# Exponentials on VectorE as four phase-shifted linear-mantissa terms, summed by the value matmul, in an attention and spectral mix

## The chip, the cores and the metric

The kernel runs on one core of a Trainium2 chip. The metric is device time in microseconds; "the time before" is the median of three runs. One profiled execution of the same kernel gives the rows below; its own time is shown beside its span.

## The reference

Two branches over the same 2048 x 448 input are mixed by a gate: softmax attention with 16 heads of width 28, and a filter in the Fourier domain.

```python
def _A_ref(x, wqkv, wo):
    H = 16; Dh = D // H                       # D = 448, S = 2048
    qkv = (x @ wqkv).reshape(B, S, 3, H, Dh)  # transposed to q, k, v of b h s d
    scores = einsum("bhqd,bhkd->bhqk", q, k) * Dh ** -0.5
    o = einsum("bhqk,bhkd->bhqd", softmax(scores), v)
    return o.reshape(B, S, D) @ wo
def _B_ref(x, w_r, w_i):
    return irfft2(rfft2(x) * (w_r + 1j * w_i))
g = sigmoid((A_x * gate_w).sum(-1))
out = g * _A_ref(A_x, ...) + (1 - g) * _B_ref(B_x, ...)
```

## The kernel before

**Tiling.** The heads are taken in four groups g of four (heads lie in 32-row strips of the 128 partitions), and the queries in four blocks c of 512. Each pair n = (g, c) is a stage; there are 16. In a stage, 16 key tiles kt of 128 keys times four heads give 64 units, a unit being the scores of one key tile and head, 128 x 512. Four units of one key tile are called a quad. The queries and keys are scaled so that a score is the logarithm to base 2 times 512 (`UNITS`), and a row of each carries half the squared norm, so that no maximum has to be subtracted; the weights `w` put that back into V.

**Who computes which exponential.** `ND[n]` quads of stage n go to VectorE (27 quads in all), the rest to ScalarE. ScalarE works in steps of three and two units, alternating between the PSUM tiles `psA` and `psB` (line 1033), and writes bf16 into a `ring` of 30 slots. VectorE's quads are "dunits": a score matmul into one of two background PSUM banks `bg`, an addition that makes a 16-bit integer `y4` of it (line 969), and when all four are there, a cubic in the mantissa over the whole quad, 128 x 2048, in seven operations (`g1` to `g7`, lines 976 to 998), the last of which writes a `pd` tile. `y4` has two buffers, `pd` four; `dF` and `dW` one.

**Value matmul.** In `attention`, the quads of a stage are read in pairs: eight matmuls (four heads, each in its own 32 output rows) accumulate into one PSUM bank `pvb`, with `vw` (V times `w`, one column for the row sum) as weights. VectorE's quads stand together, ahead of the last two of the stage. A ring slot is free again when the pair that reads it has run. After the stage, `normalise` evicts the bank (line 1124), sends the row sums through a DMA (`rs`), takes the reciprocal, sends it back in rows by two DMAs (`r8`), spreads it over the partitions by a matmul, and multiplies.

**Order of the work.** All instructions are collected as `Op`s with an engine, an assumed duration, dependencies, a due time (`key`) and a release time. `Sched.run` plays them through a list schedule and the program is emitted in the planned order, which each engine then follows strictly. Scores for ScalarE come first on PE; other PE work (projections, V blocks, the Fourier branch, out-projection, all through the two `bg` banks) goes between them by due time. Where PE would stand idle, `fill` puts a matmul of zeros into a free `bg` bank or, while a value accumulation is open, adds zeros to `pvb`; only while the busy share in a sliding stretch of the plan (`HAMW`) is under `HAMF`. DMAs go through SP's queue in the planned order, POOL sets and pads weights and casts the row-sum columns of `vw` (line 870). `proj_group`, `w_block` and `v_block` make keys, queries, `w` and `vw` of a group during the stage before it.

## Time and profile before

| | |
|---|---|
| time, median of 3 runs | 488.3 us (485.94 to 495.7) |
| profiled execution, its own time | 483.99 us |
| its span, first to last instruction | 482.2 us |
| mean granted TensorE clock | 0.943 of full speed |
| PE / VectorE / ScalarE / POOL busy | 425.6 / 401.2 / 423.8 / 22.5 us |

The span is cut by the profile into instructions of each engine. Idle time of an engine is put down to what ended it. A busy PE is not a PE at its peak, since the ends of pipelined matmuls are modelled; durations of neighbours on one engine overlap a little, so the distance between starts is the better measure of pace. The granted clock is the share of the 2.4 GHz that PE got: 0.5 is the level of 1.2 GHz.

### The profile page before, as it was taken

The numbers are of one execution on the slowest core, as the hardware profiler recorded it, in microseconds if no ns is written. First come the engines' busy times: TensorE is split into PE (matmuls) and PEld (weight loads), VectorE is DVE, ScalarE is ACT, GpSimd is POOL, SyncE is SP. The second block draws the span as 40 slices with busy tenths as digits, with TensorE's granted clock in tenths as the row PEclk, the third lists the DMA queues.
The fourth block names the chain that finished last, engine by engine and source line by source line (L and its number), as shares of the span: only waits on it lengthen the run. The fifth ranks groups of instructions, "written<-read, shape, count | busy, mean of one in ns | idle before, by whom it ended". The sixth has DMA issues, their size and how long they took to land.

```text
span 482.2 us, 8537 instructions
## 1 busy us (share of the span) xinstructions
PE 425.6 (88%) x3271; PEld 156.5 (32%) x3271; DVE 401.2 (83%) x682; ACT 423.8 (88%) x390; POOL 22.5 (5%) x58
## 2 busy tenths in 40 slices
PE   6899899898988799988888898999899889998876
PEld 3433223223443222233333333223244332322222
DVE  2555788579889968999999999799998989999732
ACT  2679999779999969999999989689999979999950
POOL 6600000000000000000000000000000000000000
PEclk9989999759999958999999999599999999999998
DMA  9110011001100211121111100000000000010011
GB/s 249 18 34 28 4 27 48 3 0 26 26 1 16 55 23 24 32 48 40 24 26 33 28 12 2 12 1 13 24 16 13 24 22 24 24 42 28 12 40 38
DMA packets 28361, 13.98 MB, mean 29 GB/s; under 512 B 18176, under 2 KB 27936, under 8 KB 28320
## 3 DMA queue, kind: packets, MB, share of 16 engines
q1 hardware_dynamic: 27216, 13.09, 10.9%
q8 instruction: 25, 0.41, 0.4%
q10 hardware_dynamic: 1104, 0.35, 0.3%
q14 instruction: 16, 0.13, 0.1%
HBM read 11.21 MB, written 1.84 MB: 27 GB/s over the span
## 4 chain that ended last, share of the span: by engine, by line
ACT 38%; PE 28%; DVE 15%; issue 13%; DMA 4%; SPq 2%; ACTq 0%; DVEq 0%
ACT ring L1033 37%; PE bg L508 13%; PE psA L508 5%; PE pvb L508 5%; PE psB L508 4%; DVE y L969 2%; SPq L490 2%; PE bg L511 2%; DVE dW L984 1%; DMA k<-nrow 1%; DMA U<-in_A_wqkv_dram 1%; DVE dF L976 1%; DMA r<-rhl 1%; DMA rs<-pvs 1%; DVE pvs L1124 1%
## 5 line engine op out<-in xcount | busy, mean ns | idle before, releaser
L1033 ACT ACTIVATE ring<-psA 128x1536 bf16<-128x1536 f32 (+1 forms) x184 | 283.8, 1542 | 22.7 <-PE psA L508 16.4
L1033 ACT ACTIVATE ring<-psB 128x1024 bf16<-128x1024 f32 x183 | 205.6, 1124 | 6.9 <-PE pvb L508 4.2
L508 PEld LDWEIGHTS <-k 32*128 32x128 bf16 x1024 | 49.5, 91 | 154.7 <-issue 142.7
L508 PE MATMUL psA<-q,k 32*128 32x512 bf16 x550 | 76.9, 400 | 25.6 <-ACT ring L1033 22.0
L508 PE MATMUL psB<-q,k 32*128 32x512 bf16 x366 | 75.3, 397 | 6.7 <-ACT ring L1033 5.3
L969 DVE TENSOR_SCALAR y<-bg 128x512 uint16<-128x512 f32 x108 | 72.2, 682 | 6.9 <-PE bg L508 6.5
L508 PE MATMUL pvb<-ring,vw 128*32 128x512 bf16 x916 | 73.4, 400 | 0.5 <-DVE pvs L1124 0.5
L508 PE MATMUL bg<-q,k 32*128 32x512 bf16 x108 | 40.3, 399 | 1.2 <-DVE k L810 0.3
L984 DVE TENSOR_TENSOR dW<-dF,dW 128x2048 f16<-128x2048 uint16 x27 | 32.8, 1214 | 0.1
L995 DVE TENSOR_TENSOR y<-y,dW 128x2048 uint16<-128x2048 uint16 x27 | 32.7, 1212 | 0.0
L991 DVE TENSOR_TENSOR dW<-dW,dF 128x2048 f16<-128x2048 f16 x27 | 32.6, 1208 | 0.1
L508 PEld LDWEIGHTS <-vw 128*32 128x32 bf16 x1024 | 17.0, 95 | 32.6 <-issue 29.2
L1228 DVE CAST U<-bg 113x512 bf16<-113x512 f32 x32 | 21.5, 682 | 3.6 <-PE bg L508 3.2
L508 PE MATMUL bg<-R,X 128*113 128x256 bf16 x128 | 23.9, 290 | 0.2 <-DVE y L969 0.2
L508 PEld LDWEIGHTS <-xT 128*128 128x128 bf16 x320 | 18.5, 97 | 16.1 <-issue 14.3
L870 POOL CAST vw<-w 128x16 bf16<-128x16 f32 x16 | 7.4, 466 | 342.2 <-ACT w L865 342.2
L508 PE MATMUL bg<-xT,wpk 128*128 128x512 bf16 (+1 forms) x60 | 22.6, 478 | 0.6 <-DVE xT L780 0.3
L810 DVE TENSOR_SCALAR k<-bg,cst 128x512 bf16<-128x512 f32 x15 | 11.2, 749 | 13.7 <-PE bg L508 13.7
L508 PE MATMUL bg<-xT,wpq 128*128 128x512 bf16 (+1 forms) x60 | 19.7, 415 | 0.4 <-DVE q L810 0.2
L1160 DVE SCALAR_TENSOR_TENSOR fin<-bg,gs,xtok 128x448 bf16<-128x448 f32 x16 | 10.9, 680 | 10.9 <-PE bg L508 10.8
L508 PE MATMUL bg<-Bd,xT 128*128 128x450 bf16 x64 | 17.2, 357 | 2.1 <-DVE X L1203 1.0
L976 DVE TENSOR_SCALAR dF<-y 128x2048 uint16<-128x2048 uint16 x27 | 18.5, 686 | 0.3
(97 smaller groups left out, 475.8 us busy)
## 6 DMA issues: line engine op xcount, KB each, us to landing
RB<-cRB SPq DMA_DIRECT2D x16, 128.0 KB
Wg<-in_B_w_i_dram SPq DMA_DIRECT2D x32, 56.2 KB
xtok<-in_A_x_dram SPq DMA_DIRECT2D x4, 448.0 KB
out_dram<-fin SPq DMA_DIRECT2D x16, 112.0 KB
CS<-cCS SPq DMA_DIRECT2D x16, 96.0 KB
Wg<-in_B_w_r_dram SPq DMA_DIRECT2D x16, 56.2 KB
r<-rhl SPq DMA_DIRECT2D x32, 4.0 KB
U<-in_A_wqkv_dram SPq DMA_DIRECT2D x2, 252.0 KB
```

What stands on the lines that cost most here:

```text
L490: self.pin(e.dma_start(out=out() if callable(out) else out, in_=in_() if callable(in_) else in_))
L508: self.pin(self.nc.tensor.matmul(out, lhsT=lhsT, rhs=rhs, start=start, stop=stop, **kw))
L511: self.pin(self.nc.tensor.transpose(out=out, in_=in_, identity=self.c("ident")[0:n, 0:n]))
L810: self.pin(nc.vector.tensor_scalar(out=dst, in0=self.bgi(it), scalar1=self.sv, scalar2=None, op0=ALU.mult))
L969: self.pin(nc.vector.tensor_scalar(out=ys[:, s, :], in0=self.bgi(it), scalar1=127 * UNITS + 1.5, scalar2=0.0, op0=ALU.add, op1=ALU.max))
L976: self.pin(nc.vector.tensor_scalar(out=fl(self.dF), in0=fl(ys), scalar1=511, scalar2=None, op0=ALU.bitwise_and))
L984: self.pin(nc.vector.tensor_tensor(out=fl(self.dW), in0=fl(self.dF), in1=fl(self.dW), op=ALU.mult))
L991: self.pin(nc.vector.tensor_tensor(out=fl(self.dW), in0=fl(self.dW), in1=fl(self.dF).bitcast(F16), op=ALU.mult))
L995: self.pin(nc.vector.tensor_tensor(out=fl(ys), in0=fl(ys), in1=fl(self.dW), op=ALU.add))
L1033: self.pin(nc.scalar.activation(out=self.ring[:, u0:u0 + len(st), :], in_=slot[:, 0:len(st), :], func=ACT.Exp, scale=LN2 / UNITS))
L1160: self.pin(nc.vector.scalar_tensor_tensor(out=fin[:], in0=self.bgi(it)[:, 0:D], scalar=self.gs[:, t:t + 1], in1=self.bm[:, t, 0:D], op0=AL ...
L1228: self.pin(nc.vector.tensor_copy(out=dst, in_=src))
```

## The change

VectorE's exponential no longer corrects the mantissa by a cubic. The integer y, read as a floating-point number, is a linear interpolation of the exponential between powers of two. The change makes four such numbers from each quad, with y shifted by 0, 129, 258 and 387 of 512 units (`PHASE`), and lets the value matmul sum all four, with weights `vd` that are `vw` times a gain for each phase (`PHGAIN`). So a VectorE quad costs four wide operations where there were seven, and is read four times by PE where it was read once. In detail:

- `ND` becomes 0, then 2 fourteen times, then 1: 29 quads where there were 27.
- The phases of a stage's quads are spread over the stage by `self.elems`; the first comes after three quads in the first stage of a group, else after one. `pd` gets six buffers, `dF` and `dW` go.
- `vd` (for the last three key tiles, `DKT`) is made once for a group: `v_block` for the last block evicts part of the tile in f32 to `vf` by a second VectorE operation, POOL copies the weights' column and makes four products. These wait for the last phase matmul of the group before.
- The weights of group 3 (`wpad`) share the tile of group 0, and are padded after its projections.
- `fill` uses at most 256 columns, a limit of 0.7 where it was 0.62, and may write the value bank between its eviction and the next stage, and, as it did, while it is open. The prologue's fillers become 20 of 256 columns.
- Due times: `DUE_P`, and `SWP` names a constant that stays 1.0.

```diff
-EXPA, EXPB = 0.29727136, 0.09245069
+PHASE = (0, 129, 258, 387)
+PHGAIN = [2.0 ** (-d / UNITS) / (4 * 1.0406815) for d in PHASE]
+NPD, DKT = 6, 3
...
-HAMW, HAMF = 3.4, 0.62
+HAMW, HAMF = 3.4, 0.7
...
-            n = min(512, int((gap - SWITCH) * 2400.0) // 32 * 32)
+            n = min(256, int((gap - SWITCH) * 2400.0) // 32 * 32)
...
             elif pvopen[0]:
+                target = None
+            elif pvopen[1] is not None and pvopen[1].end is not None and pvopen[1].end + LAT["DVE"] <= t:
+                target = -1
+            elif pvopen[1] is not None and pvopen[1].end is None:
                 target = None
...
-    ND = [0] + [1] * 2 + [2] * 12 + [1]
+    ND = [0] + [2] * 14 + [1]
...
-        self.dF = T([P, 4, 512], U16, "dF")
-        self.dW = T([P, 4, 512], F16, "dW")
-        self.pd = [T([P, 4, 512], BF16, f"pd{i}") for i in range(4)]
+        self.pd = [T([P, 4, 512], BF16, f"pd{i}") for i in range(NPD)]
+        self.vd = T([P, 4, DKT, 4, 32], BF16, "vd")
+        self.vf = T([P, DKT, 4, DH + 1], F32, "vf")
...
+        for i in range(20):
+            self.pe(256, lambda: self.mm(self.psA[:, 2, 0:256], self.zero[:, 0:P], self.zero[:], True, True),
...
+        elif bank < 0:
+            self.mm(self.pv[:, 0:n], self.zero[:, 0:P], self.zero[:, 0:n], True, True)
...
+        lo = 4
+        if b == 3:
+            alld = min(len(self.dk[4 * g + c]) for c in range(4))
+            lo = 4 - min(alld, DKT)
...
-        e = self.dve(0.54, fe, [ops[-1], wop[0], self.vms[g], ("vwar", g)] + pre, due - 1.5, free=it)
+        e = self.dve(0.07 + lo * .117, fe, [ops[-1], wop[0], self.vms[g], ("vwar", g)] + pre, due - 1.5,
+                     free=it if b < 3 else None)
+        if b == 3:
+            def fd():
+                src = free_dims(self.bgi(it), [[m, DKT], [DH, 4], [1, DH]], m * (4 - DKT))
+                wv = free_dims(self.w[g][:], [[4, DKT], [1, 4], [0, DH]], 16 * b + 4 * (4 - DKT))
+                self.pin(nc.vector.tensor_tensor(out=self.vf[:, :, :, 0:DH], in0=src, in1=wv, op=ALU.mult))
+            e2 = self.dve(0.07 + DKT * .117, fd, [e] + getattr(self, "vdprev", []), due - 1.4, free=it)
+
+            def fw():
+                self.pin(nc.gpsimd.tensor_copy(out=self.vf[:, :, :, DH:DH + 1],
+                                               in_=free_dims(self.w[g][:], [[4, DKT], [1, 4], [1, 1]],
+                                                             16 * b + 4 * (4 - DKT))))
+            pw = self.pool(0.2, fw, [wop[0]] + getattr(self, "vdprev", []), due)
+            self.vdops[g] = []
+            for f in range(4):
+                def fp(f=f):
+                    self.pin(nc.gpsimd.tensor_scalar(out=self.vd[:, f, :, :, 0:DH + 1], in0=self.vf[:],
+                                                     scalar1=PHGAIN[f], scalar2=None, op0=ALU.mult))
+                self.vdops[g].append(self.pool(0.6, fp, [e2, pw, self.vdms], due))
+            self.vdready[g] = self.vdops[g][-1]
+            self.vdprev = self.vdops[g]
...
+        for n in range(16):
+            quads = [("a", kt) for kt in self.ak[n]]
+            na, ph = len(quads), [("d", kt, f) for kt in self.dk[n] for f in range(4)]
+            lo = 3 if n % 4 == 0 else 1
+            el = []
+            for i, q in enumerate(quads):
+                while ph and lo + (na - 2.0 - lo) * (4 * len(self.dk[n]) - len(ph)) / (4 * len(self.dk[n])) <= i:
+                    el.append(ph.pop(0))
+                el.append(q)
+            el[-1:-1] = ph
+            self.elems.append(el)
...
+                due = fdue[0] - DUE_P + 0.6 * s
+                m = sc.op("PE", 0.22, fm, self.kev[g, kt // 4] + self.qev[g, c], due - 1, rel, "row", it, name="dunit")
...
-                    self.pin(nc.vector.tensor_scalar(out=ys[:, s, :], in0=self.bgi(it), scalar1=127 * UNITS + 1.5,
+                    self.pin(nc.vector.tensor_scalar(out=ys[:, s, :], in0=self.bgi(it), scalar1=127 * UNITS,
                                                      scalar2=0.0, op0=ALU.add, op1=ALU.max))
-                p1s.append(self.dve(0.61, f1, [m, prevy], due - 12, free=it))
...
-            def g1(ys=ys):
-                self.pin(nc.vector.tensor_scalar(out=fl(self.dF), in0=fl(ys), scalar1=511, scalar2=None,
-                                                 op0=ALU.bitwise_and))
...
-            def g2():
-                self.pin(nc.vector.tensor_scalar(out=fl(self.dW), in0=fl(self.dF), scalar1=-512.0, scalar2=1.0 / 512,
-                                                 op0=ALU.add, op1=ALU.mult))
...
-            def g3():
-                self.pin(nc.vector.tensor_tensor(out=fl(self.dW), in0=fl(self.dF), in1=fl(self.dW), op=ALU.mult))
...
-            chain = p1s + [prevt]
-            for j, (fn, dur) in enumerate([(g1, .61), (g2, .61), (g3, 1.14), (g4, .61), (g5, 1.14), (g6, 1.14)]):
-                o = self.dve(dur, fn, chain, due - 4 + j * .3, name="dexp")
-                chain = [o]
-            o = self.dve(0.61, g7, chain + [pvdep.get(di - 4)], due, name="dexp")
-            self.dlast[di] = o
-            self.pdops[n, kt] = (o, pds, di)
+                p1s.append(self.dve(0.61, f1, [m, prevy], due, free=it, name="dp1"))
...
+            for f in range(4):
...
+                pds = self.pd[j % NPD]
...
+                def g1(ys=ys, pds=pds, f=f):
...
+                    self.pin(nc.vector.tensor_scalar(out=fl(pds).bitcast(U16), in0=fl(ys), scalar1=float(PHASE[f]),
+                                                     scalar2=0.25, op0=ALU.add, op1=ALU.mult))
+                o = self.dve(0.61, g1, p1s + phs[-1:], fdue[f], name="dexp")
+                phs.append(o)
+                pdseq.append((o, n, kt, f))
+                self.pdops[n, kt, f] = (o, pds, j)
...
-            quads = [("a", kt) for kt in self.ak[n]]
-            dqs = [("d", kt) for kt in self.dk[n]]
-            pos = len(quads) - 2
-            quads[pos:pos] = dqs
+            quads = self.elems[n]
...
+                            if kind == "a":
+                                rhs, lw = self.ring[:, self.unit_slot[n, kt, s][0], :], self.vw[g][:, kt, s, :]
+                            else:
+                                rhs = self.pdops[n, kt, f[0]][1][:, s, :]
+                                lw = self.vd[:, f[0], kt - (NT - DKT), s, :]
+                            self.mm(self.pv[32 * s:32 * s + 32, :], lw, rhs,
```

## Rows read from the trace of the kernel before

**Rows 1.** The page's first part: busy time, share of the span, instructions.

```profile
PE 425.6 (88%) x3271; PEld 156.5 (32%) x3271; DVE 401.2 (83%) x682; ACT 423.8 (88%) x390; POOL 22.5 (5%) x58
```

**Rows 2.** The timeline of ScalarE: start, duration (us), instruction, idle time before it.

```profile
314.60 1.02 ACT L1033 ACTIVATE ring<-psB 128x1024 bf16<-128x1024 f32 x1 [3.12 <-PE pvb L508]
...
455.07 1.52 ACT L1033 ACTIVATE ring<-psA 128x1536 bf16<-128x1536 f32 x1
...
457.31 1.54 ACT L1033 ACTIVATE ring<-psA 128x1536 bf16<-128x1536 f32 x1
...
464.01 0.77 ACT L1033 ACTIVATE ring<-psA 128x512 bf16<-128x512 f32 x1
```

**Rows 3.** Busy by stretch: length, PE, PEld, DVE, ACT, POOL, clock, DMA share, GB/s.

```profile
36.00:90.00 54.00, 49.70 (x377) 16.30 (x374) 39.77 (x66) 52.95 (x49) 0.51 (x2) 1.00 0.10 25
90.00:108.00 18.00, 17.66 (x78) 3.81 (x79) 11.35 (x16) 12.29 (x11) 0.00 (x0) 0.53 0.00 1
108.00:168.60 60.60, 52.21 (x482) 22.30 (x481) 55.81 (x101) 60.60 (x59) 1.71 (x4) 1.00 0.11 25
168.60:183.00 14.40, 14.37 (x64) 3.09 (x63) 9.56 (x16) 9.97 (x9) 0.00 (x0) 0.53 0.09 19
183.00:301.40 118.40, 103.63 (x862) 40.41 (x858) 116.27 (x212) 115.05 (x106) 2.81 (x4) 0.99 0.12 27
301.40:314.00 12.60, 12.60 (x60) 3.89 (x62) 10.04 (x16) 8.29 (x7) 0.00 (x0) 0.51 0.04 12
314.00:466.00 152.00, 136.66 (x1114) 49.47 (x1107) 138.47 (x222) 145.10 (x132) 1.82 (x4) 1.00 0.08 22
```

**Rows 4.** Waits of ScalarE: total us, times, longest us.

```profile
ACT ring L1033 <- PE pvb L508: 10.2, 6, 3.1
```

**Rows 5.** The timeline of all engines around one wait for the ring.

```profile
269.42 0.61 PE L508 MATMUL pvb<-ring,vw 128*32 128x512 bf16 x8
...
280.10 0.63 DVE L998 TENSOR_SCALAR pd<-y 128x2048 uint16<-128x2048 uint16 x1
...
281.61 0.61 PE L508 MATMUL pvb<-pd,vw 128*32 128x512 bf16 x8
...
282.96 1.45 ACT L1033 ACTIVATE ring<-psA 128x1536 bf16<-128x1536 f32 x1 [2.29 <-PE pvb L508]
```

**Rows 6.** Groups by line: tiles, shapes, count, busy us, mean ns, idle before.

```profile
L969 DVE TENSOR_SCALAR y<-bg 128x512 uint16<-128x512 f32 x108 | 72.2, 682 | 6.9 <-PE bg L508 6.5 <-PE psB L508 0.3
...
L984 DVE TENSOR_TENSOR dW<-dF,dW 128x2048 f16<-128x2048 uint16 x27 | 32.8, 1214 | 0.1
...
L976 DVE TENSOR_SCALAR dF<-y 128x2048 uint16<-128x2048 uint16 x27 | 18.5, 686 | 0.3
```

**Rows 7.** The timeline of PE at full clock, one value op and its successor.

```profile
46.69 0.61 PE L508 MATMUL pvb<-ring,vw 128*32 128x512 bf16 x8
...
47.23 0.39 PE L508 MATMUL psA<-q,k 32*128 32x512 bf16 x3
```

**Rows 8.** Busy time by stretch, matmuls of zeros alone (fillers).

```profile
36.00:90.00 54.00, 0.00 (x0) 0.00 (x0) 0.00 (x0) 0.00 (x0) 1.00 0.10 25
...
sum 430.00, PE 21.57 PEld 5.93 ACT 0.00 POOL 0.00; mean PE 3.08 PEld 0.85 ACT 0.00 POOL 0.00
```

**Rows 9.** The timeline of PE's weight loads where the first slow stretch begins.

```profile
90.01 0.10 PEld L508 LDWEIGHTS <-cst 8*128 8x128 bf16 x1 [1.67 <-DMA r<-rhl]
```

**Rows 10.** Groups by line of POOL, the widest copy.

```profile
L598 POOL COPY wpq<-U 128x336 bf16<-128x336 bf16 x3 | 1.4, 466 | 0.3 <-DMA U<-in_A_wqkv_dram 0.3
```

**Rows 11.** The timeline of VectorE: a value bank's eviction, the last V block's.

```profile
365.45 0.68 DVE L1124 COPY pvs<-pvb 128x512 f32<-128x512 f32 x1
...
373.26 0.62 DVE L902 TENSOR_TENSOR vw<-bg,w 128x448 bf16<-128x448 f32 x1
```

**Rows 12.** The timeline of POOL: two of the sixteen equal casts.

```profile
38.05 0.25 POOL L870 CAST vw<-w 128x16 bf16<-128x16 f32 x1 [8.45 <-ACT w L865]
...
245.90 1.13 POOL L870 CAST vw<-w 128x16 bf16<-128x16 f32 x1 [5.89 <-ACT w L865]
```

More of the change, by code (lines that the diff above doesn't have):

```diff
@@ L153 @@
 SWITCH = 0.1
-HAMW, HAMF = 3.4, 0.62
+HAMW, HAMF = 3.4, 0.7
+DUE_P = 4.0
+SWP = 1.0
 class Sched:
@@ L291, in finish @@
                     pvopen[0] = not o.n
+                    if o.n:
+                        pvopen[1] = o.step
             o.start, o.end = t0, t0 + dur
@@ L796, in proj_group @@
     def proj_group(self, w, g, blocks, due, rel):
+        if not hasattr(self, "pj0"):
+            self.pj0 = {"k": [], "q": []}
         nc = self.nc
@@ L940, in attention @@
                 self.v_block(g, b, d0 + 6 + 4.0 * b, wop, d0 - 15)
+        for w, ops in self.lastpad:
+            for o in ops:
+                o.deps += self.pj0[w]
         self.dunit_ops = []
-        self.pdops = {}
+        self.elems = []
+        for n in range(16):
[9 more added lines that the diff above has]
+            self.elems.append(el)
+        self.pdops, self.pv_last = {}, {}
+        pdseq, quadl = [], []
         di = 0
-        self.dlast = {}
-        pvdep = {}
-        self.pv_last = {}
         dlist = [(n, kt) for n in range(16) for kt in self.dk[n]]
@@ L950, in attention @@
             g, c = self.groups[n]
[L951 to L956 removed]
+            el = self.elems[n]
+            fdue = []
+            for f in range(4):
+                i = el.index(("d", kt, f))
+                t = self.tstart[n]
+                for e in el[:i]:
+                    if e[0] == "a":
+                        t = max(t, self.T[self.unit_step[n, e[1], 3]])
+                fdue.append(t + 1.0)
+            rel = fdue[0] - 60.0
+            ys = self.y4[di % 2]
+            prevy = quadl[di - 2][1][-1] if di >= 2 else None
             p1s = []
@@ L986, in g4 @@
-            def g4():
-                self.pin(nc.vector.tensor_scalar(out=fl(self.dF).bitcast(F16), in0=fl(self.dF), scalar1=EXPB / 512,
-                                                 scalar2=EXPA, op0=ALU.mult, op1=ALU.add))
-            def g5():
-                self.pin(nc.vector.tensor_tensor(out=fl(self.dW), in0=fl(self.dW), in1=fl(self.dF).bitcast(F16),
-                                                 op=ALU.mult))
-            def g6(ys=ys):
-                self.pin(nc.vector.tensor_tensor(out=fl(ys), in0=fl(ys), in1=fl(self.dW), op=ALU.add))
@@ L1005, in attention @@
-            self.dlast[di] = o
-            self.pdops[n, kt] = (o, pds, di)
+                p1s.append(self.dve(0.61, f1, [m, prevy], due, free=it, name="dp1"))
+            phs = []
+            for f in range(4):
+                j = len(pdseq)
+                pds = self.pd[j % NPD]
+                def g1(ys=ys, pds=pds, f=f):
+                    fl = lambda t: t[:].rearrange("p a b -> p (a b)")
+                    self.pin(nc.vector.tensor_scalar(out=fl(pds).bitcast(U16), in0=fl(ys), scalar1=float(PHASE[f]),
[4 more added lines that the diff above has]
+                self.pdops[n, kt, f] = (o, pds, j)
@@ L1007, in attention @@
+            quadl.append((p1s, phs))
             di += 1
-            pvdep[di - 1] = ("later", n, kt)
         exps = []
@@ L1058, in attention @@
                 tk = 0.0
-                for kind, kt in pair:
+                for kind, kt, *f in pair:
                     deps += self.vready[g, kt // 4]
@@ L1077, in attention @@
                 prev_pv = o
-                for kind, kt in pair:
+                for kind, kt, *f in pair:
                     if kind == "a":
@@ L1091, in attention @@
                     e.deps.append(r)
-        for (n, kt), (o, pds, di) in self.pdops.items():
-            o.deps = [d for d in o.deps if not isinstance(d, tuple)]
-            if di >= 4:
-                o.deps.append(pd_reader[di - 4])
+        for o, pds, j in self.pdops.values():
+            if j >= NPD:
+                o.deps.append(pd_reader[j - NPD])
+        for g in range(1, 4):
+            for o in self.vdops[g]:
+                o.deps.append(self.vdlast.get(g - 1))
+                o.deps = [d for d in o.deps if d is not None]
         kr = {g: [] for g in range(4)}
```

57 lines of the change are left out of this document (27 added, 30 removed).

## The prediction

> **What bounds the kernel now.** I read the page's engine line first [rows 1]: PE, ScalarE and VectorE are all busy for 83 to 88% of the span, so no share names the bound. The timeline of ScalarE comes next [rows 2]. One pair of exponential steps (three units of 512 columns, then two) repeats every 457.31 - 455.07 = 2.24 us with no idle time between, so a unit costs 0.448 us. The 916 units of before need 916 x 0.448 = 410 us at that pace; the last step ends at 464.01 + 0.77 = 464.8 us. Wherever ScalarE is never idle, it is the bound, and nothing done elsewhere shortens that stretch.
>
> So the question is where it is idle. The table by stretch [rows 3] cuts 36 to 466 us at the places where the granted TensorE clock changes. Three stretches stand at a clock of 0.51 to 0.53 (the 1.2 GHz level); there PE is busy all the time while ScalarE idles for 18.00 - 12.29 = 5.7, 14.40 - 9.97 = 4.4 and 12.60 - 8.29 = 4.3 us: 14.4 us. In the four stretches at full clock it idles 1.05, 0.0, 3.35 and (464.8 - 314 - 145.10 =) 5.7 us: 10.1 us. Together 24.5 us.
>
> The waits of ScalarE [rows 4] give the second cause: a ring slot that is not free, because the value matmul (pvb) which reads it has not run, 10.2 us in 6 waits. One of the six is followed in [rows 5]. The value matmuls stand still from 269.42 to 281.61 us, 12.2 us, because the next one in the plan reads a pd tile, and stands in PE's order behind the chain that VectorE finishes at 280.10 + 0.63 us; the ring's 30 slots hold 30 x 0.448 = 13.4 us of exponentials, they fill, and ScalarE waits 2.29 us. VectorE has no air there: in the stretch around it, it is busy for 116.27 of 118.40 us [rows 3]. So the cubic is late, and VectorE is the second bound.
>
> **The change, part by part.** *VectorE.* A quad (one key tile, four heads) costs four additions out of PSUM, three tensor_tensor and four wide tensor_scalar operations [rows 6] (one row for each of the three kinds): 4 x 0.682 + 3 x 1.214 + 4 x 0.686 = 9.1 us. After it: the same additions and four wide tensor_scalar of the same kind, 4 x 0.682 + 4 x 0.686 = 5.5 us. Over 27 quads before and 29 after this is 246 against 159 us, so 87 us leave a VectorE that was busy for 401. The split of one V eviction per group adds at most one operation of the size of such an addition, 4 x 0.68 = 2.7 us. In the 118 us of that full stretch lie some 9.3 quads (two per 25.5 us); 34 of its 116 us go, which leaves a load of 70%. VectorE stops being a bound.
>
> *ScalarE.* Two more quads leave it: 8 units x 0.448 = **-3.6 us**, which counts fully, as it is the bound.
>
> *Ring waits.* The two pd quads of a stage stood together just ahead of its last two quads; now their eight phases are spread over it, each needs one wide VectorE operation, and no long chain holds all later value matmuls. Of the 10.2 us, 3.12 end the third slow stretch [rows 2] and are counted there; 7.1 us lie at full clock. Bounds: 0 (the waits move elsewhere) and -10.1 us (all idle time at full clock goes). I take **-7.1**, the waits whose chain I can follow.
>
> *PE.* A value matmul op of two quads takes 47.23 - 46.69 = 0.54 us to the start of the next instruction at full clock [rows 7]. Before: 256 quads, 8 ops in each of 16 stages, 128 ops. After: 16 + 14 x 22 + 19 = 343 quads, 8 + 14 x 11 + 10 = 172 ops. 44 x 0.54 = 24 us more; the 8 further score matmuls are free beside a score of ScalarE's, at most 8 x 0.54 = 4.3 us alone. What room is there? In the full-clock stretches PE is idle for 4.3 + 8.4 + 14.8 + 15.3 = 43 us [rows 3], and of the 21.6 us of filler nearly all lies there [rows 8]: some 62 us against 24 to 28. It fits as a whole, but not from 36 to 90 us: there PE has 4.3 us idle and no filler, and two stages with six more ops bring 3.2, with lone scores up to 7.5 us. I put **+1.5 us** there, between 0 and 3.2.
>
> *Clock.* The first slow stretch begins where PE stands still for a weight load that waits 1.67 us for the transfer of the reciprocals [rows 9]. What is planned now has 24 us more matmul, a filler limit of 0.7 in place of 0.62, and two more places to write fillers. That speaks for fewer slow stretches. But the transfers issued on SP are not changed, so a late r8 can stop PE as at 90 us, and once low, the clock stayed low for 12 to 18 us with PE busy for 17.66 of 18 us [rows 3]. I take one slow stretch in place of three. It costs 4.8 us (their mean) and more than before: 15 us hold 15/430 of the added 24 us, 0.8, which at half clock is 1.7. So 6.5 - 14.4 = **-7.9 us**; bounds -14.4 and +5 (three, each dearer).
> The Trainium skill (TensorE: Matmul & The Clock Gate, Part 1) says that the throttled clock is the default state and activity releases it; by that alone the added matmuls would hold the clock up throughout and the sum would be 460.4, but the trace shows a busy PE that stays at the low level for many microseconds, which is why I keep one.
>
> *What costs nothing.* The prologue's 20 fillers of 256 columns equal 10 of 512. The weights of group 3 are padded later, in the tile of group 0, but are needed some 200 us on; their copies on POOL take 0.47 us and less [rows 10]. New filler targets only use gaps; a filler that writes the value bank waits for its eviction, which the next value matmul does anyway. No DMA is added. On POOL come 16 products of 348 elements and four small copies; see the rivals.
>
> *Start of a group.* The first phase matmul of a group comes after three quads, and its weights come from the eviction of the group's last V block. In the kernel before, that eviction ends 373.26 + 0.62 - 365.45 = 8.4 us after the preceding stage's value bank is evicted (the worst of three [rows 11]); four products of 0.47 us follow it, 10.3 us, while three quads take 3 x 4 x 0.448 = 5.4 us. The value matmuls would stand still for 4.9 us at three group starts. The ring hides this if they are not already 8 us behind. Bounds 0 and 3 x 4.9 = 15 us; I take 0, because the ring is longer and V evictions will queue behind a lighter VectorE.
>
> *Sum.* 483.99 (profiled run: span 482.2 and 1.8 around it) - 3.6 - 7.1 + 1.5 - 7.9 = 466.9, so **467 us**. That run lies 4.3 us under the median of the three runs, 488.3; I take part of that spread for slow stretches that differ from run to run, so that with fewer of them the runs lie closer together, and I don't add it.
>
> **Rivals.** *The clock drops as often as before.* For: SP's queue and the r8 transfers are the same, and the low level holds long. Against: more matmuls. Then 484.0 - 3.6 - 7.1 + 1.5 + 3 x 1.7 = 479.9 us.
>
> *The waits move to the starts of the groups.* For: V evictions are late before, and a longer chain now hangs on them. Against: a ring of 13.4 us. It costs the upper bound above: 467 + 15 = 482 us.
>
> *POOL holds the value matmuls: slower.* PE runs in order. The products may overwrite their tile only after the last phase matmul of the group before. Between that and the first one of the next group lie six quads of exponentials, 6 x 4 x 0.448 = 10.8 us, in which four products must be done: from 2.7 us each it costs, and behind the waiting matmul stand the scores, so ScalarE stops two steps later. Price of one: the copy of 336 elements takes 0.47 us [rows 10]; on the other side, the cast of 16 elements takes 0.25 us at one time and 1.13 at another [rows 12], and at its shortest per element a product would take 0.25/16 x 348 = 5.4 us. At the first price four take 1.9 us and all is hidden; at the last 21.8, three group changes cost 3 x 11.0 = 33 us, and the time is 500 us. I take the first, whose shape (strips of 28 in a row) is nearly that of the product.
> The spread of the small cast fits a rule of the Trainium skill (SBUF — State Buffer, Who interferes with whom): VectorE in its two-port modes and GpSimd lock each other out for whole instructions. By that each product could wait for one wide operation too, 4 x (0.47 + 0.69) = 4.6 us in all, still under 10.8; it raises this rival's chance a little.
>
> *PE has no room after all.* If the 24 us fell wholly on ScalarE's path with no clock gained: 484.0 - 3.6 + 24 = 504 us. Against it: 62 us of room.
>
> **How the numbers follow.** Forecast (fewer slow stretches, ring waits gone) 0.60, its own range 456 (nothing idle after 36 us, 484.0 - 3.6 - 24.5) to 474. Clock as before 0.17, 474 to 486, a third of it under the bound. Waits at the group starts 0.12. POOL 0.07, PE 0.04. About 2% is what a measurement of this kernel can tell from no change: faster is below 478.5, slower above 498. So faster 0.60 + 0.06 = 0.66; same 0.11 + 0.12 = 0.23; slower 0.07 + 0.04 = 0.11. The range goes from 455 to 482: it leaves out the slower cases and the upper parts of the two middle ones, under 2 in 10.
>
> **What would show it.** VectorE near 315 us busy and no cubic rows, ring waits behind pvb under 3 us, the ring's pair still at 2.24 us, at most one stretch at the low clock, and ScalarE idle for some 10 us after 36 us: right. Three low stretches: the first rival. Value matmuls that stand still at the three group starts, behind V or a POOL product: the second or the third. If the pair itself gets longer than 2.24, ScalarE's pace was not what I took it for, and the whole floor is wrong.

## The result, and the profile after

| | before | after |
|---|---|---|
| time, median of 4 runs | 487.12 us (485.75 to 495.7) | 458.34 us (457.46 to 462.05) |
| profiled execution, its own time | 483.99 us | 457.46 us |
| its span | 482.2 us | 455.7 us |
| mean granted TensorE clock | 0.943 | 0.989 |

The ratio is 0.9433, with a 95% interval of 0.9357 to 0.9508: faster. The forecast was 467 us in a range of 455 to 482, so the direction and the range held, and the time itself was 9 us too high. The sum behind it was right in only some of its terms. Averages further down take all executions of a kernel, fast and slow; by the fast ones alone the mean spans are 481.0 us (18 executions of the kernel before) and 456.4 (8 of the changed one), and of the 24.6 us between them 13.4 are clock and 11.2 the rest, in place of 15.8 and 11.4.

The engine line of the page (busy us, share of the span, instructions), which answers [rows 1]:

```profile
PE 416.1 (91%) x3661; PEld 164.9 (36%) x3678; DVE 327.9 (72%) x621; ACT 416.9 (91%) x386; POOL 39.5 (9%) x75
```

VectorE lost 73 us. PE reads 343 quads in place of 256 and yet is busy for 9.5 us less; less of its time lies at the lower clock (mean 0.989 for 0.943). ScalarE is busy for 91% of a shorter span.

The same seven stretches of time as in [rows 3] (length, PE, PEld, DVE, ACT, POOL, clock, DMA share, GB/s; the last one cut at 441 us, where the exponentials have ended):

```profile
36.00:90.00 54.00, 51.36 (x428) 16.95 (x428) 40.74 (x74) 53.11 (x49) 5.61 (x9) 1.00 0.12 32
90.00:108.00 18.00, 16.66 (x113) 5.45 (x117) 15.07 (x27) 18.00 (x17) 0.00 (x0) 1.00 0.01 2
108.00:168.60 60.60, 55.98 (x569) 23.48 (x570) 50.09 (x108) 58.05 (x57) 6.14 (x9) 1.00 0.16 34
168.60:183.00 14.40, 12.43 (x112) 4.41 (x110) 13.41 (x27) 14.40 (x14) 0.00 (x0) 1.00 0.20 45
183.00:301.40 118.40, 107.64 (x1003) 41.56 (x1009) 99.74 (x195) 118.38 (x109) 6.41 (x9) 1.00 0.10 22
301.40:314.00 12.60, 12.47 (x83) 4.26 (x83) 9.63 (x17) 12.60 (x13) 0.00 (x0) 1.00 0.05 13
314.00:441.00 127.00, 119.72 (x1082) 46.59 (x1080) 79.66 (x143) 124.35 (x114) 6.37 (x9) 0.99 0.09 24
```

The three stretches that stood at half clock now show 1.00, and ScalarE has no idle time in them. From 183 to 301.4 us it idles 0.02 us where it idled 3.35, and VectorE's load there is 99.74 of 118.40 us (84%; I had worked out 70%).

ScalarE's waits over its exponentials, 36 to 441 us (total us, times, longest us), to be read beside [rows 4]:

```profile
ACT ring L1081 <- PE psA L518: 2.9, 3, 1.4
ACT ring L1081 <- PE pvb L518: 2.8, 2, 1.8
```

Two more rows of the kernel before, from 36 to 466 us:

```profile
ACT ring L1033 <- PE psA L508: 10.9, 14, 1.4
...
ACT ring L1033 <- PE psB L508: 2.2, 4, 0.9
```

Ring waits behind the value matmul went from 10.2 us to 2.8. Waits for a score matmul on psA and psB were 13.1 us and are 2.9; by the timeline 11.8 of the 13.1 lay in the three slow stretches, so in my sum they stand under the clock. ScalarE's timeline shows where the run starts, the larger ring wait, and the pace:

```profile
19.10 1.45 ACT L1081 ACTIVATE ring<-psA 128x1536 bf16<-128x1536 f32 x1 [1.02 <-PE psA L518]
...
111.23 1.45 ACT L1081 ACTIVATE ring<-psA 128x1536 bf16<-128x1536 f32 x1 [1.76 <-PE pvb L518]
...
433.94 1.71 ACT L1081 ACTIVATE ring<-psA 128x1536 bf16<-128x1536 f32 x1
435.28 1.28 ACT L1081 ACTIVATE ring<-psB 128x1024 bf16<-128x1024 f32 x1
436.20 1.71 ACT L1081 ACTIVATE ring<-psA 128x1536 bf16<-128x1536 f32 x1
437.54 1.28 ACT L1081 ACTIVATE ring<-psB 128x1024 bf16<-128x1024 f32 x1
438.45 1.71 ACT L1081 ACTIVATE ring<-psA 128x1536 bf16<-128x1536 f32 x1
```

A pair takes 436.20 - 433.94 = 2.26 us; over all pairs without a wait the median is 2.24 us before and 2.25 after. The pace of ScalarE is the same, so what was gained on it is idle time, and eight units. From the first exponential to the end of the last one, ScalarE idled 4.5 us up to 36 us and 24.5 after that (14.4 in the slow stretches, 10.1 at full clock); now it is 2.6 and 5.3. It is busy there for 6.9 us less, 3.6 of which are the eight units; the rest is probably that an exponential before a wait overlaps no successor. The stretch behind the last exponential is 1.9 us shorter (17.4 to 15.5), and the first exponential is 3.4 us later. That makes up the 26.5 us between the two profiled spans.

### The profile page after: what moved, and what is told of

Read it like the earlier page. It is cut to its first block, busy times and chain, and to the rows that moved or that the text cites. A ratio compares the mean times of both kernels' runs of the same rounds, so it can differ in the third digit from the quotient of the medians.

```text
span 455.7 us, 9292 instructions
## 1 busy us (share of the span) xinstructions
PE 416.1 (91%) x3661; PEld 164.9 (36%) x3678; DVE 327.9 (72%) x621; ACT 416.9 (91%) x386; POOL 39.5 (9%) x75
## 4 chain that ended last, share of the span: by engine, by line
ACT 48%; PE 28%; issue 12%; DVE 7%; DMA 3%; SPq 1%; ACTq 0%; DVEq 0%
ACT ring L1081 48%; PE bg L518 11%; PE pvb L518 6%; PE psA L518 5%; PE psB L518 4%; PE bg L521 2%; DVE pd L1050 1%; DVE y L1040 1%; DMA U<-in_A_wqkv_dram 1%; DMA r<-rhl 1%; DMA rs<-pvs 1%; DVE U L1282 1%; SPq L500 1%; ACT w L890 0%; DVE pvs L1178 0%
## 5 line engine op out<-in xcount | busy, mean ns | idle before, releaser
L1081 ACT ACTIVATE ring<-psA 128x1536 bf16<-128x1536 f32 x182 | 294.2, 1616 | 6.9 <-PE psA L518 5.1
L1081 ACT ACTIVATE ring<-psB 128x1024 bf16<-128x1024 f32 x181 | 216.2, 1194 | 1.2 <-PE pvb L518 1.1
L518 PE MATMUL psA<-q,k 32*128 32x512 bf16 x546 | 72.2, 383 | 19.7 <-ACT ring L1081 15.4
L518 PE MATMUL pvb<-ring,vw 128*32 128x512 bf16 x908 | 80.6, 385 | 0.1
L1050 DVE TENSOR_SCALAR pd<-y 128x2048 uint16<-128x2048 uint16 x116 | 79.1, 697 | 0.8 <-PE pvb L518 0.2
L518 PE MATMUL pvb<-pd,vd 128*32 128x512 bf16 x464 | 46.3, 386 | 0.1
L1178 DVE COPY pvs<-pvb 128x512 f32<-128x512 f32 x16 | 11.0, 684 | 14.9 <-PE pvb L518 14.8
L951 POOL TENSOR_SCALAR vd<-vf 128x348 bf16<-128x348 f32 x16 | 19.8, 1238 | 17.0 <-DVE vf L940 16.0
L518 PE MATMUL bg<-Bd,ZT 113*128 113x448 bf16 x64 | 17.8, 356 | 0.2 <-DVE ZT L1376 0.2
L518 PEld LDWEIGHTS <-zero 128*128 128x128 bf16 x154 | 14.6, 104 | 9.2 <-issue 5.5
L518 PEld LDWEIGHTS <-X 128*113 128x113 bf16 x128 | 13.1, 130 | 12.5 <-issue 12.4
```

Source lines behind the costliest of these rows:

```text
L518: self.pin(self.nc.tensor.matmul(out, lhsT=lhsT, rhs=rhs, start=start, stop=stop, **kw))
L951: self.pin(nc.gpsimd.tensor_scalar(out=self.vd[:, f, :, :, 0:DH + 1], in0=self.vf[:], scalar1=PHGAIN[f], scalar2=None, op0=ALU.mult))
L1050: self.pin(nc.vector.tensor_scalar(out=fl(pds).bitcast(U16), in0=fl(ys), scalar1=float(PHASE[f]), scalar2=0.25, op0=ALU.add, op1=ALU.mult))
L1081: self.pin(nc.scalar.activation(out=self.ring[:, u0:u0 + len(st), :], in_=slot[:, 0:len(st), :], func=ACT.Exp, scale=LN2 / UNITS))
L1178: ev = self.dve(0.61, lambda: self.pin(nc.vector.tensor_copy(out=pvs[:], in_=self.pv[:])), [last, self.nlast[i]], -100.0)
```

## The clock is taken out of a comparison

The granted clock differs between executions of one kernel (0.900 to 0.960 in the kernel before), and that blurs differences of a few us. Each execution's mean granted clock c is known, and there are two levels, so 2(1 - c) of its span lay at the lower one. The 28 executions of the kernel before that ran beside the others go from a span of 474.5 us at 0.960 (38 us low) to 494.3 at 0.900 (99 us low): 19.8 us of span for 61 us, 0.32 for one; a straight line through all of them gives 0.29, and the profile before 14.4 us of idle ScalarE in 45 us [rows 3], 0.32. Lines through the few executions of the other kernels give 0.26 to 0.47. I use 0.3, and call span - 0.3 x 2(1 - c) x span the span at equal clock. It is an estimate, but within a kernel it varies with a standard deviation of 0.3 to 1.3 us where the spans themselves vary by up to 20. Between kernels whose low-clock time differs by 40 to 50 us, the choice of 0.3 itself matters by some 2 us.

| kernel | executions | mean span | mean us at the low clock | span at equal clock |
|---|---|---|---|---|
| before | 28 | 483.7 | 64.7 | 464.2 |
| after (with a_copy) | 8 | 456.4 | 12.0 | 452.8 |
| b_fill: before, new fillers | 4 | 470.3 | 26.6 | 462.3 |
| b_lin: before, no cubic | 4 | 459.7 | 27.2 | 451.6 |
| b_pv4: before, pd read four times | 4 | 516.2 | 79.2 | 492.4 |
| a_oldfill: after, old fillers | 4 | 466.7 | 30.4 | 457.6 |
| a_pv1: after, one phase read | 4 | 456.7 | 21.3 | 450.3 |
| a_dve2: after, wide operations twice | 10 | 483.5 | 14.4 | 479.2 |
| a_nd27: after, 27 quads | 4 | 457.4 | 14.0 | 453.2 |
| a_late: after, phases together | 4 | 459.5 | 15.4 | 454.9 |
| a_both, a_vdrel: after, other prologue | 8 | 457.1 | 13.3 | 453.1 |
| a_ph2n3: after, two phases, 41 quads | 4 | 467.3 | 34.2 | 457.1 |

So the 27.3 us between the mean spans are 0.3 x (64.7 - 12.0) = 15.8 us of clock and 11.4 us of everything else (with 0.26 or 0.35 in place of 0.3, the rest is 13.6 or 8.9).

## The experiments

A ratio is the time of the run over that of the kernel before, run beside it.

**b_fill: the new filler settings alone, in the kernel before.**

```diff
-HAMW, HAMF = 3.4, 0.62
+HAMW, HAMF = 3.4, 0.7
-            n = min(512, int((gap - SWITCH) * 2400.0) // 32 * 32)
+            n = min(256, int((gap - SWITCH) * 2400.0) // 32 * 32)
...
+            elif pvopen[1] is not None and pvopen[1].end is not None and pvopen[1].end + LAT["DVE"] <= t:
+                target = -1
...
```

> The kernel before with the planner's new filler settings alone (share limit 0.7, 256 columns at most, the value bank as a target between its eviction and the next stage). If the fillers are what keeps TensorE's clock up, the three slow stretches after 36 us go and 14 us with them: about 470 us, with the 7 us of ring waits still there. If the late VectorE is what starves PE, or if it takes real matmuls, at least two slow stretches stay: 480 to 490 us. My theory says the second.

Measured: 473.38 us (466.48 to 474.97), beside 487.28 (476.3 to 494.39) for the kernel before. The theory that I leaned to was wrong. The low clock fell to 26.6 us; at equal clock 1.9 us are gained, which is within what the choice of 0.3 can make. Ring waits stay, with VectorE as full as before (399.9 us busy). ScalarE's waits over the whole execution (from 36 us on the first row is 4.5 us in 10):

```profile
ACT ring L1039 <- PE psA L512: 8.6, 14, 1.4
ACT ring L1039 <- PE pvb L512: 6.8, 4, 2.8
```

So the fillers alone bring about half of the change's gain (13.4 of 27.3 us between mean spans), nearly all through the clock.

**b_lin: the cubic left out of the kernel before.** VectorE's quads are the linear interpolation alone (a coarser output); fillers, quads and value matmuls are those of before.

```diff
-            for j, (fn, dur) in enumerate([(g1, .61), (g2, .61), (g3, 1.14), (g4, .61), (g5, 1.14), (g6, 1.14)]):
+            for j, (fn, dur) in enumerate([]):
```

> The kernel before without the six operations of the cubic (the exponential stays linear between powers of two, so the output is coarser): VectorE loses 27 x 5.7 = 154 us, PE's work stays as it was. If VectorE's lateness makes both the ring waits and the starved PE, both go: 462 to 468 us and a clock of 1.0 after 36 us. If the clock needs the added matmuls, only the 7 us of ring waits go and slow stretches stay: 474 to 480 us. My theory leans to the second, since I gave the clock's part to the added matmuls.

Measured: 461.90 us (458.02 to 464.2). VectorE is busy for 273.1 us, and no wait of ScalarE for a ring slot is left. Its waits from 36 us to the end, all of them:

```profile
ACT ring L1031 <- PE psA L506: 4.4, 5, 2.5
ACT ring L1031 <- PE bg L506: 1.7, 3, 0.9
```

At equal clock it is 12.6 us under before: as much as the whole 11.4 us that the change gains there. And although no matmul was added and the filler settings are those of before, the low clock fell from 64.7 us to 27.2. In this kernel a lighter VectorE gives both, 24.0 of the change's 27.3 us between mean spans; my theory leaned the other way.

**b_pv4: each pd quad read four times, in the kernel before** (its weight in the sum is four times too large).

```diff
-                        for s in range(4):
+                        for s in list(range(4)) * (1 if kind == "a" else 4):
```

> The kernel before with its cubic, but each VectorE quad is read four times by the value matmul (so its weight in the sum is four times too large): PE gets 81 more quads, 22 us, as in the change, and VectorE stays full. If the added matmuls hold the clock, the slow stretches go and the ring waits stay: 468 to 474 us. If the clock falls because VectorE starves PE, they stay and the added work makes them dearer: 485 to 495 us. My theory: the first.

Measured: 517.87 us (508.86 to 527.39). The ring waits grew to 46.3 us in 15, with 79.2 us at the low clock. Neither theory had foreseen it. It does not measure the price of the added matmuls alone: two quads read four times stand in one unbroken op late in the stage, behind the cubic. What it shows is that more matmuls do not by themselves hold the clock.

**a_oldfill: the changed kernel with the old filler settings** (the edit of b_fill backwards).

> The changed kernel with the filler settings of before (limit 0.62, up to 512 columns, no value bank between stages). If the new settings hold the clock, slow stretches come back: 465 us or more. If they are a side matter, it stays within 3 us of 458 with a clock of 1.0 in most of the span. My theory: the second.

Measured: 467.12 us (466.62 to 473.19), 8.8 above after. The low clock rises to 30.4 us, which is 5.5 of it; 4.8 us remain at equal clock, and the ring waits behind pvb are 6.3 us in 4. The filler settings are needed in the changed kernel too; I had taken them for a side matter. Beside b_lin, which has the same old settings and reads one term where this reads four, it is 6.0 us longer at equal clock. This kernel also has 53 us more work on VectorE, other due times and another order of the value matmuls, so which of these costs the 6.0 us is open.

**a_pv1: of the four phases only the first is read by the value matmul** (three terms are left out of the sum; VectorE makes them all the same).

```diff
-                        for s in range(4):
+                        for s in (range(4) if kind == "a" or f[0] == 0 else ()):
```

> The changed kernel with one phase of each VectorE quad read by the value matmul in place of four (three of the four terms are left out of the sum): PE loses 87 of its 343 value quads, 24 us, VectorE's work stays. If the added matmuls help to hold the clock, low-clock time grows from 3 us to 15 or more and the time goes to 462 us or more. If they are only a burden that PE's slack covers, the time stays within 2 us of 458; if they burden ScalarE, it falls to 452 to 455. After the first four runs my theory is the second: the light VectorE and the new fillers hold the clock.

Measured: 459.05 us (454.56 to 461.33), ratio 0.9468 (0.9385 to 0.955). Without the three further reads the span at equal clock is 2.5 us shorter, but 21.3 us lie at the low clock in place of 12.0, which costs 2.8. With the new filler settings the added value matmuls are free in sum: they cost what they buy. In the traces zeros take 31.6 us of PE in this kernel and 20.1 in after, since the plan fills the gaps that are left; with the fillers of after the low clock might have been longer still. That was not run.

**a_dve2: each wide VectorE operation issued twice** in the changed kernel, without the branch of `fill` that adds zeros between a stage's last value matmul and its eviction.

```diff
+                    for _ in range(2):
+                        self.pin(nc.vector.tensor_scalar(out=fl(pds).bitcast(U16), in0=fl(ys), scalar1=float(PHASE[f]),
...
-                o = self.dve(0.61, g1, p1s + phs[-1:], fdue[f], name="dexp")
+                o = self.dve(1.22, g1, p1s + phs[-1:], fdue[f], name="dexp")
```

> The changed kernel with each wide VectorE operation issued twice (the same values into the same tile): VectorE gets 116 x 0.69 = 80 us back and is as full as before, PE and the fillers stay as changed. If VectorE's relief is the main gain, ring waits and low-clock time come back: 470 to 485 us. If the new order of the value matmuls and the fillers are the gain, it stays under 463. My theory: the first.

Measured: 485.48 us (482.99 to 487.19), ratio 1.0038 (1.0005 to 1.0071): with VectorE as busy as before, all the gain is gone, as my theory had it. Its engine line, and ScalarE's wait for ring slots:

```profile
PE 435.4 (90%) x3723; PEld 169.9 (35%) x3737; DVE 399.4 (83%) x737; ACT 421.9 (87%) x386; POOL 40.6 (8%) x75
```

```profile
ACT ring L1080 <- PE pvb L516: 20.7, 13, 7.8
```

But the low clock, which the theory wanted back too, did not come: 14.4 us are low, where after has 12.0. So nearly all of the 26.4 us at equal clock are waits: from 36 us to the last exponential ScalarE idles 30.2 us, in after 5.3. It is even 15 us over before at equal clock. I read this so: with a full VectorE, the eight phases that PE needs over a stage hold the value matmuls more often than two quads at its end do (13 ring waits for 6). The experiment shows which way VectorE's load works and not how much the change saved.

**a_nd27: the changed kernel with the quads of before**, without the same branch of `fill`.

```diff
-    ND = [0] + [2] * 14 + [1]
+    ND = [0] + [1] * 2 + [2] * 12 + [1]
```

> The changed kernel with 27 VectorE quads, as before, in place of 29 (and without the filler in the moment between the last value matmul and its eviction): ScalarE gets 8 units back. If ScalarE's pace is the bound, 458.3 + 3.6 = 462 us. If PE is the bound, six value quads fewer make it 456 to 458.

Measured: 460.21 us (456.02 to 460.45), ratio 0.9502 (0.9445 to 0.956). At equal clock it is 453.2 against 452.8 us: the eight units that ScalarE gave up are worth 0.4 us, not 3.6, and both theories were off. The profiles of this kernel and of a_copy, both at a mean clock of 0.992, both have a span of 454.2 us, and their first exponential at 16.30 and 16.29 us; ScalarE is busy for 3.4 us more here (420.3 against 416.9), idles 2.5 us less between its first and last exponential (6.4 against 8.8), and ends 0.9 us later (439.3 against 438.3); the stretch behind its end is 0.9 us shorter.

**a_late: the phases stand together ahead of a stage's last two quads**, as the cubic's quads did.

```diff
-            lo = 3 if n % 4 == 0 else 1
+            lo = na - 2.0
```

> The changed kernel with the eight phases of a stage standing together just ahead of its last two quads, as the cubic's quads stood before, in place of being spread over the stage. Nothing is left out. Theory that spreading the phases took away the ring waits: the value matmuls again stand still for the last phase, ring waits behind pvb come back by 7 to 10 us, and the time is 465 to 469. Theory that the lighter VectorE did it (its operations are done long before they are read): ring waits stay at 3 to 5 us, and the time is 457 to 461. With all eight phases in a row, PE would run four ops of value matmul back to back, 2.2 us, ahead of the scores; as a step of three and two units lasts 2.24 us, a part of that may fall on ScalarE: at most 15 x 1 us.

Measured: 460.61 us (460.39 to 463.65), ratio 0.9586 (0.9544 to 0.9627); after, run beside it (a_copy), 458.15. The ring waits:

```profile
ACT ring L1081 <- PE pvb L518: 6.4, 4, 2.8
```

So of the 7.4 us of ring waits that went, 3.6 come back when the phases stand together, and 2.1 us of time at equal clock. The larger part of the 11.4 us is not the order of the phases; b_lin puts it down to VectorE's load.

**a_both and a_vdrel: the prologue.** a_both has the prologue's fillers of before (10 of 512) and clears `vd` at another place; there it comes behind the memset of `vw` and ends at 7.91 us, and the copies of x start no earlier (8.06 us). a_vdrel releases it 14 us later:

```diff
-            self.vd[:].rearrange("p f a b c -> p (f a b c)"), 0.0)), (), -90)
+            self.vd[:].rearrange("p f a b c -> p (f a b c)"), 0.0)), (), -90, 14.0)
```

> The changed kernel with the prologue's fillers of before (ten of 512 columns) and the clearing of vd moved behind POOL's other clearing. In the changed trace the first exponential starts at 19.10 us, before at 15.66. If POOL's clearing of vd holds up VectorE's first copies and the clock falls in the pause, the first exponential comes back to about 15.7 and the time is 454 to 455 us. If the late start has another cause, 457 to 459.

> The changed kernel with one memset on POOL released 14 us later (the one that clears vd), nothing else. Theory: in the changed kernel that memset runs from 4.69 to 6.07 us and pushes the second memset of vw to 7.92; VectorE's copy of the projection weights takes 1.87 us for that time where it took 0.58 before, and all that follows is 0.6 us later. With the memset moved, that copy should take about 0.6 us, begin after 4.9 to 6.7 us as before, and ScalarE's first ring step should begin at about 15.7 us where it was 19.1 (and 16.3 in runs with the same prologue but full clock there). Time: 458.3 - 0.6 to 458.3 - 3.4, so 455 to 458. Rival: it is not the memset but the fillers of 256 columns or the clock: then the first step stays at 16.3 to 19.1 and the copy may be short all the same.

Measured: a_both 460.80 us (455.27 to 463.38), ratio 0.9497 (0.9411 to 0.9582); a_vdrel 458.16 us (453.4 to 461.65), ratio 0.9487 (0.94 to 0.9574). POOL and VectorE of after, where the weights are copied:

```profile
4.69 1.38 POOL L750 MEMSET vd<- 128x1536 bf16 x1
6.01 1.91 POOL L747 MEMSET vw<- 128x2048 bf16 x1
```

```profile
6.09 1.87 DVE L611 COPY wpk<-U 64x112 bf16<-64x112 bf16 x1
6.29 1.76 DVE L608 COPY wpq<-U 128x336 bf16<-128x336 bf16 x1
...
8.06 0.49 DVE L650 COPY xT<-psB 128x512 bf16<-128x512 bf16 x1
```

VectorE and ScalarE of a_vdrel:

```profile
6.52 0.58 DVE L611 COPY wpk<-U 64x112 bf16<-64x112 bf16 x1
...
7.21 0.49 DVE L650 COPY xT<-psB 128x512 bf16<-128x512 bf16 x1
```

```profile
15.45 1.45 ACT L1081 ACTIVATE ring<-psA 128x1536 bf16<-128x1536 f32 x1 [1.02 <-PE psA L518]
```

The same copy takes 1.87 us and ends at 7.96, when the memset of `vw` ends (7.92), or takes 0.58 in a_vdrel, where only a memset of 128 x 512 (0.62 us) runs beside it; the copies of x follow 0.85 us earlier, and so does the first exponential (15.45 against 16.29 in a_copy). That much is shown. The 0.85 us does not show in the medians, 458.16 beside 458.15, nor at equal clock, 452.7 beside 452.6.

**a_copy: the changed kernel once more, beside a_vdrel, a_late and a_ph2n3.**

> The changed kernel itself, unchanged, on the chip and in the call of the runs beside it. Theory that the clock in the prologue differs from run to run with one and the same program: the profile may show ScalarE's first ring step at 16.3 where it was 19.1, with a full clock from 9.7 to 16 us; the times stay at 455 to 462. Rival, the low clock there belongs to this program: 19.1 again, clock about 0.5 there.

Measured: 458.15 us (456.13 to 459.33), ratio 0.9516 (0.9479 to 0.9552). From 9.5 to 16 us, in the columns of the table by stretch, first after and then a_copy:

```profile
9.50:16.00 6.50, 5.49 (x13) 1.85 (x13) 0.18 (x1) 1.19 (x2) 2.98 (x10) 0.50 0.69 158
```

```profile
9.50:16.00 6.50, 4.73 (x36) 2.53 (x35) 1.62 (x4) 1.65 (x3) 2.81 (x9) 1.00 0.60 146
```

One program, two levels of the clock: the first exponential starts at 19.10 us in one and at 16.29 in the other. So of the 3.4 us by which after starts later than before (15.66), 2.8 are a clock that differs from run to run, and the other 0.6 are of the size of what a_vdrel gives back.

**a_ph2n3: a candidate.** Two phases in place of four (a coarser sum), three quads of most stages on VectorE, and the memset of a_vdrel.

```diff
-PHASE = (0, 129, 258, 387)
+PHASE = (0, 256)
-    ND = [0] + [2] * 14 + [1]
+    ND = [0] + [2] * 2 + [3] * 12 + [1]
```

> A candidate: two phases (0 and 256) in place of four, so the sum is a coarser exponential, and three quads of most stages on VectorE in place of two (41 in all for 29); vd cleared later as in the run beside it. ScalarE gives up 48 units, 48 x 0.448 = 21.5 us; PE reads 215 + 82 = 297 quads where it read 343, 23 ops less, 23 x 0.54 = 12.4 us; VectorE has 48 more additions and 34 fewer wide operations, 48 x 0.69 - 34 x 0.70 = 9 us more. Theory that ScalarE's own work is the floor of the changed kernel: 458.3 - 21.5 - 0.6 = 436, within 432 to 442. Rival, PE's order and the two background banks bind (91% busy, 48 score matmuls more that go through two banks beside the projections): the pair of exponential steps gets gaps, ScalarE idles 15 us more, 445 to 455.

Measured: 469.49 us (458.69 to 478.78). Even the shortest of its four executions is no faster than after's median (458.15 beside it), though ScalarE has 20 us less to do; both theories were off. The other three had a clock of 0.936 to 0.970, and at equal clock it is 4.3 us over after. Its waits, in the execution with the highest clock (0.996, span 456.9 us):

```profile
ACT ring L1081 <- PE pvb L518: 24.3, 14, 3.3
```

One of the 14, in the timeline of all engines:

```profile
226.01 1.42 DVE L1040 TENSOR_SCALAR y<-bg 128x512 uint16<-128x512 f32 x2
...
227.65 1.28 DVE L1050 TENSOR_SCALAR pd<-y 128x2048 uint16<-128x2048 uint16 x2
...
228.77 0.40 PE L518 MATMUL pvb<-pd,vd 128*32 128x512 bf16 x4
...
229.48 1.45 ACT L1081 ACTIVATE ring<-psA 128x1536 bf16<-128x1536 f32 x1 [3.26 <-PE pvb L518]
```

Between 220.8 and 228.8 us no value matmul ran, only zeros. The next one reads a pd tile; its additions `y` reach VectorE one or two at a time through the two bg banks, between V blocks and the Fourier branch, and the last are done at 227.4. VectorE is busy for only 73%: it is not full, it is fed late. No kernel here with the whole sum of four terms is measurably faster than the changed one.

## Why the prediction was right, and where its sum was not

- **VectorE is the second bound, and the change lifts it: right.** b_lin and a_dve2 show it from both sides: without the cubic 12.6 us go at equal clock, with a full VectorE 26.4 come (in a plan that waits for it more often). VectorE's size was nearly right: 327.9 us busy for a forecast of 315. The wide operation is 697 ns and the addition 686, as in [rows 6], and by the sums of such rows 86 us went; but durations of neighbours overlap, and `vf` and the prologue's copies take a little more, so in busy time that is 73. Its load from 183 to 301 us came to 84% and not 70% for another reason too: the kernel gets on faster, and the same stretch holds 39 additions where it held 33.
- **Ring waits, -7.1 us: right in place, too large in size.** All ring waits fell from 10.2 to 2.8 us [rows 4], under the 3 that I had allowed. But 3.1 of the 10.2 end the third slow stretch and I had counted them under the clock; at full clock 7.1 became 2.8, which is -4.3, and all of ScalarE's idle time at full clock after 36 us went from 10.1 to 5.3. That so few are left is due to VectorE's load (b_lin has none) and, by a_late, in part the order of the phases.
- **What no term held.** Of the 11.4 us at equal clock, the units brought 0.4, the added matmuls took 2.5 and the later start of the exponentials 0.6; what is left, 11.4 - 0.4 + 2.5 + 0.6 = 14.1 us, is twice my term for waits. It is a remainder and was not measured wait by wait; b_lin's 12.6 supports its size. The profiles find 4.8 us of it as idle time at full clock, 1.9 as idle time before 36 us (in part clock), 1.9 behind the last exponential, and 3.3 as busy time of ScalarE beyond the eight units. I had counted none of the last three.
- **Eight units, -3.6 us: wrong.** a_nd27 gives 0.4. The step said that a unit taken from ScalarE "counts fully, as it is the bound"; that holds only where ScalarE is never idle. After 36 us it idles 3.8 us with 27 quads and 6.3 with 29 (a_copy): the wait for something else takes up most of what is saved. a_ph2n3 drives it further: 48 units less, and the waits ate them all.
- **Early crowding of PE, +1.5 us: did not happen there.** From 36 to 90 us ScalarE idles 0.89 us, before 1.05 [rows 3]. The whole cost of the added matmuls is 2.5 us at equal clock (a_pv1), inside the bounds of 0 to 3.2 but not in that stretch alone.
- **Clock, -7.9 us: right in sign, half the size, and for the wrong reason.** It is worth 15.8 us on the mean of the executions: 52.7 us less at the low clock. In the profile no slow stretch longer than 4 us is left after 36 us, where I kept one of 15, and all 14.4 us of idle time in slow stretches went, my lower bound. I credited the added matmuls first. They keep 9.3 us from being low (a_pv1), worth 2.8, which they cost again. The filler settings keep 18.4 to 38 us (a_oldfill, b_fill), and in the kernel before the lighter VectorE does as much by itself (b_lin). The two overlap: either alone leaves 27 us low, both without the added matmuls 21 (a_pv1), all three 12. Once fillers and matmuls are there, VectorE's load hardly counts for the clock: a_dve2 has 14.4 us low.
- **The prologue, priced at nothing: wrong.** I looked at the fillers there and at the copies of `wpad`, but not at the memset that clears the new tile `vd`. It moves the first exponential by 0.6 to 0.85 us; that the whole kernel gets longer by it no run shows. By the Trainium skill (SBUF — State Buffer, Who interferes with whom), a copy of VectorE in a two-port mode and an instruction of GpSimd lock each other out for whole instructions. The copy and the memset that end together at 7.9 us agree; in which mode the copy ran, no row shows.
- **POOL's product, 0.47 us: wrong by a factor of 2.6, without effect.** A group of POOL by line:

```profile
L951 POOL TENSOR_SCALAR vd<-vf 128x348 bf16<-128x348 f32 x16 | 19.8, 1238 | 17.0 <-DVE vf L940 16.0
```

  Four take 4 x 1.238 = 4.95 us, under the 10.8 from which I said that they would hold the value matmuls. The nearest row in shape was not the nearest in kind: it copied bf16, this reads f32 and multiplies. No wait of PE for a product stands in the profile.
- **Group starts, 0: right.** Two ring waits are left, 1.76 us at 111.23 and 1.08 at 370.00, and neither stands at the start of a group.
- **The rivals.** The clock did not drop as often as before (479.9), the waits did not move to the group starts (482), POOL did not hold the value matmuls (500), and PE had room (504).

In sum: 27.3 us between the mean spans where I had 17.1. Of the 10.2 missing, 7.9 are the clock and 7.0 (14.1 for 7.1) what waits were worth; against them stand 3.2 for the units, 0.6 for the prologue and 1.0 for the matmuls (2.5 for 1.5). That this adds up to within 0.1 is no test, since the 14.1 are a remainder. The forecast came within 9 us in part because errors of both signs met.

Open is how VectorE's load and the clock hang together: in the kernel before, a lighter VectorE left less time at the low clock (b_lin), but in the changed kernel a full one brought hardly any back (a_dve2). By which pauses of PE it works was not found. Nor was b_lin run with the new fillers, or the due times and the six `pd` buffers by themselves.

## What to carry to other kernels

When three engines are all near 85%, a lighter one is worth what the others wait for it, here some 11 us at equal clock for 73 us of its work, and taking work off the busiest can be worth little once it waits, here 0.4 us of 3.6. Where the clock differs between executions, bring each to equal clock by its own mean before two versions are compared; differences of 2 us that medians of four runs blur become plain, as long as the low-clock times are alike. A new tile's memset in the prologue can hold up another engine: look at what runs beside it.

## What the runs showed of the hardware

- The clock between 9.5 and 16 us was 0.50 in one execution of the same program and 1.00 in another, which moved the first exponential by 2.8 us. A profile of one execution can't say to which version a low clock belongs.
- A us at the low clock cost about 0.3 us of span, not one: 14.4 us of idle ScalarE in 45 us [rows 3], 19.8 us of span in 61 us over 28 executions. In the prologue, 6.5 us at the low clock delayed the first exponential by 2.8.
- A 64 x 112 copy on VectorE took 1.87 us beside a memset of 128 x 2048 on POOL and ended with it, and 0.58 beside one of 128 x 512.
